# Linear attention with a squared-ReLU feed-forward on one core: a new token tiling, k.v in 64-row pairs, GpSimd taking early products, and a new order

## The chip, the core and the metric

The kernel runs on one core of a Trainium2 chip. A core has TensorE (PE: matmuls from SBUF into PSUM; its weight loads are shown apart as PEld), VectorE (DVE), ScalarE (ACT), GpSimd (POOL) and SyncE (SP, which here only issues DMAs), each with its own instruction stream, and 16 DMA engines that move data between DRAM and SBUF. The metric is the device time of one execution in microseconds (us), the median of the runs of a kernel.

## What is computed

Eight batches of eight heads, 576 tokens and 64 features per head go through an attention with an exponential feature map; its output, 4608 tokens of 512 features, goes through a feed-forward part.

```python
def phi(x):
    proj = np.einsum('bhsd,df->bhsf', x, w_phi)            # 64 -> 128
    proj = proj - np.max(np.abs(proj), axis=-1, keepdims=True)
    return np.concatenate([np.exp(proj), np.exp(-proj)], axis=-1)
q_p, k_p = (phi(q), phi(k))
kv = np.einsum('bhsf,bhsd->bhfd', k_p, v)
z = np.sum(k_p, axis=2)
num = np.einsum('bhsf,bhfd->bhsd', q_p, kv)
den = np.einsum('bhsf,bhf->bhs', q_p, z)[..., None] + 1e-06
attn = num / den
x = attn.transpose(0, 2, 1, 3).reshape(B * S, H * D)       # 4608 x 512
h = np.maximum(x @ w_in, 0.0)                              # 512 -> 2048
out = h * h @ w_out                                        # 2048 -> 512
```

Inputs and output are float32 in DRAM; the loads, issued by POOL, turn them into bfloat16 in SBUF.

## The kernel before

**Tiles of tokens.** A batch has 576 = 512 + 64 tokens per head. The 512 lie on the 128 partitions as token 4p + j (`load`, L245: runs of four tokens, 1024 bytes; `load_q`, L265: two halves of two tokens, 512 bytes). The last 64 tokens of each head are a part of their own ("s", L253), for two heads on the two halves of the partitions. From batch 2 on, the loads go out piece by piece (`PIECES`).

**Stages of a batch** (`attention(b)`).
- k and q are transposed. For the batches 0 and 1 PE does it (`pe_transposes`, L307, with a copy out of PSUM by DVE or ACT, L190 and L192); for the others SP issues a crossbar transpose in the DMA (`transposed`).
- `project` (L333; L360 for k of batch 0, L482 for q of batch 0) multiplies by `w_phi`, the token tile being the stationary operand. A matmul uses 64 of the 128 rows, one head; two heads stand on the two halves. DVE takes the maxima of the absolute values (L367, L388, L489), ACT the exponentials of k (L376, L394).
- The maxima of k go into v: ACT writes `exp(-max)` and `exp(max)` into two extra columns of `va` (`em_ops`, L407 and L413), DVE multiplies v by them (`v_ops`, L421).
- `kv_ops` multiplies `kp`, `kn` and `va`: per pair of heads 16 matmuls with 128 rows (tokens) and 65 columns (L449) and two with 130 columns for the part "s" (L454, on `va` columns of which half are zeros from a memset at the start). A copy takes the result to SBUF.
- `q_ops` projects q with `w_phi` as the stationary operand (L524), two exponentials follow (L539). In batch 0 all eight heads of 128 tokens are taken at once, which puts the eight matmuls on the same half of the rows.
- `out_ops` multiplies q's features with kv for eight heads (L554), positive part, scale by `en` on DVE (L566), negative part, reciprocal (L574), normalise into `xo` (L578). `xo` is transposed into `xT`: by PE in batch 0 (L594, copies L603), else by a DMA transpose that SP issues (L612). The 64 left tokens of a batch go to `xS`.

**Feed-forward.** Chunks 0 to 7 of 512 tokens are the batches' tiles, chunk 8 is `xS`. `ffn_in` (L692; `ffn_in_small`, L703, by 128 tokens in chunk 0) gives h, `relu_sq` takes it out of PSUM by ACT (L669) or DVE (L671), 512 columns each, and DVE squares it (L678). `ffn_out` (L757; L721 for the very last tile, in two halves) gives the output, a copy goes to `ot`, SP stores it (L772, L775).

**Order.** Every step is an `Op` with an engine; the functions only collect them. `ORDER` is the list of their numbers in the order of issue, and with it the order in each engine's stream; it was worked out ahead by a planner from the costs in `add`, and `STATES` says which of two engines takes an operation that `plan.either` offers to both. `BASES` gives the PSUM banks. `GATES` makes some loads wait for a named operation, `FILL` puts matmuls on a constant tile (L825) ahead of certain operations. `pin` ties each engine to this order. So the engines run in their own streams and wait for each other's results through semaphores.

Of the kernel before, what the change touches and what calls it, by code (L numbers as in the profile page):

```python
# [7 lines left out]
F32 = mybir.dt.float32  # L8
# [7 lines left out]
SEM = 0.045  # L16
# [8 lines left out]
def dve_cost(n):  # L25
    return n / 960 + 0.064, n / 960 + 0.150 + SEM

# [80 lines left out]
def kernel(  # L108
# [60 lines left out]
    kv_sb = ring("kv", 2, [4, 2, 2, D1])  # L169
    NQP = 3  # L170
    NXT = 2
    assert B * S == NCH * TCH and NCH == B + 1 and S == TCH + 64
# [3 lines left out]
    xT = [ring(f"xT{c}", 2, [4, 2, P]) for c in range(NXT)]  # L176
    xS = sb("xS", [4, KC, P])
    mkn = sb("mkn", [36], F32)
    hr = ring("hr", 4, [TCH])
# [13 lines left out]

    def ps1(g):
        return psum[:, g.base, :]
# [3 lines left out]


    PIECES = ((0, 1), (1, 2), (2, 3), (3, 4))

    LD = {"main": 2.85, "s": 0.3, "w": 2.85}

    def late(b, tag=""):
        return "ld" if b >= 2 else "v0" if b == 0 and tag == "xv" else "first"

    def work(b, x):  # L210

        return x + 0.1 if b >= 2 else x
# [21 lines left out]
    for b in range(2):  # L234
        for sg in range(2):
            def fn(b=b, sg=sg):
                pin(nc.vector.memset(va[b][sg][:, 32:40, :], 0.0))
            add("DVE", (0.49, 0.6), fn, w=[("ve", b, sg, 4, hi) for hi in range(2)], what="zero")

    def load(src, dst, b, tag, prs=((0, 4),), single=True, release=False):  # L240

        x = dst[b % 2]
        for a, z in prs:
            def fn(a=a, z=z):
                pin(nc.gpsimd.dma_start(  # L245
                    out=x[:, a * 512 : z * 512].rearrange("p (h x) -> p h x", x=4 * D),
                    in_=src[b][2 * a : 2 * z, 0:512, :].rearrange("h (p j) d -> p h (j d)", j=4)))
            add("POOL", (0.72, 0), fn, w=[(tag, b % 2, pr) for pr in range(a, z)],
                dma=(work(b, LD["main"] * (z - a) / 4), SW_IN, "ld", late(b, tag)), release=release, what=tag)
        if single:  # L250
            for hi in range(2):
                def fn(hi=hi):
                    pin(nc.gpsimd.dma_start(  # L253
                        out=x[hi * 64 : hi * 64 + 64, 2048:2304].rearrange("p (pr d) -> p pr d", d=D),
                        in_=src[b][hi::2, 512:576, :].rearrange("pr p d -> p pr d")))
                add("POOL", (0.72, 0), fn, w=[(tag, b % 2, "s", hi)], dma=(LD["s"], SW_IN, "ld", late(b)),
                    release=release, what=tag + "s")

    def load_q(b, jjs=(0, 1), single=True, release=False, prs=((0, 4),)):

        x = xq[b % 2]
        for jj in jjs:
            for a, z in prs:
                def fn(jj=jj, a=a, z=z):
                    pin(nc.gpsimd.dma_start(  # L265
                        out=x[:, jj * 1024 + a * 256 : jj * 1024 + z * 256].rearrange("p (h x) -> p h x", x=128),
                        in_=q[b][2 * a : 2 * z, 0:512, :].rearrange("h (p j) d -> p h (j d)", j=4)[:, :, jj * 128 : jj * 128 + 128]))
                add("POOL", (0.72, 0), fn, w=([("xq", b % 2, jj)] if z == 4 else []) + [("xq", b % 2, jj, y) for y in range(a, min(z, 3))],
                     dma=(work(b, LD["main"] / 8 * (z - a)), SW_IN, "ld", late(b)), release=release, what="xq")
        if single:  # L270
            load(q, xq, b, "xq", prs=(), release=release)

    def of(tag, b, us):
        qs = [("xq", b % 2, u, a) for u in us if u != "s" for a in range(3)] if tag == "xq" else []
        return qs + [(tag, b % 2, u) for u in us if u != "s"] + [(tag, b % 2, "s", hi) for u in us if u == "s" for hi in range(2)]

    def load_win(i):
        def fn():
            pin(nc.gpsimd.dma_start(
                out=win[i], in_=moe_w_in[:, i * 512 : (i + 1) * 512].rearrange("(kc p) m -> p kc m", p=P)))  # L280
        add("POOL", (0.72, 0), fn, w=[("win", i)], dma=(LD["w"], SW_IN, "ld", "first"), what="win")

    def load_wout(i):
# [3 lines left out]
        add("POOL", (0.72, 0), fn, w=[("wout", i)], dma=(LD["w"], SW_IN, "ld", "first"), what="wout")  # L287
# [6 lines left out]

    def attention(b):
        s2 = b % 2
        pe_in = b < 2
# [3 lines left out]
        def pe_transposes(x, tag, ttag, blocks, srcs, view):  # L301
# [6 lines left out]
            add("PE", pe_cost(n, 0.056), fn, r=of(tag, b, srcs) + ["ident"], opens=g, w=[g], what="T" + tag)  # L308
            def fn():
                i_ = ps1(g).bitcast(BF16)[:, : n * P].rearrange("p (i c) -> p i c", c=P)  # L310
# [4 lines left out]
        def transposed(x, xt, tag, ttag):  # L315
            def fn():
                pin(nc.sync.dma_start_transpose(out=xt, in_=x))
            add("SP", (2.8 if tag == "xk" else 3.4, 0), fn, r=of(tag, b, (0, 1, "s") if tag == "xq" else (0, 1, 2, 3, "s")),
                w=[(ttag, s2, t) for t in range(18)], dma=(3.6, HW_IN, "x", "kq"), what="X" + tag)
# [659 lines left out]
```

## Time and profile before

| | |
|---|---|
| median of 3 runs | 362.51 us (361.58 to 363.54) |
| span of the profiled execution | 358.8 us |
| granted clock of TensorE, mean | 0.997 |
| DMA queue of POOL (loads) | 51744 packets, 18.36 MB, 48.4% of 16 engines' span |
| DMA queue of SP (transposes, stores) | 50608 packets, 20.55 MB, 26.4% |
| POOL's own loads issued | 162, about 0.76 us each |

The span runs from the first to the last instruction of the profiled execution; the time of a run is longer, as it has the launch and the end around it. In the tables of groups a row gives line, engine, operation, operands and shapes, the number of instructions, their busy time in us, the mean of one in ns, and the idle time of the engine just before them with what ended it. A busy PE counts matmuls in flight, which overlap, so their mean (380 ns for 512 columns) is longer than the time from one start to the next (four L757 in 0.86 us). In tables by stretches, each engine has its busy time in that stretch and its number of instructions, then the granted clock, the DMA engines' busy share and GB/s. In the chain of waits and in the order of instructions, the first number is the start in us, the second the length.

### The profile page before, as it was taken

Reading aid. Unit: us, or ns where it says so; the run is one execution under the profiler, and the core shown is the slowest. Engines: PE = TensorE matmul, PEld = TensorE weight load, DVE = VectorE, ACT = ScalarE, POOL = GpSimd, SP = SyncE. Lnnn points to the kernel's source line nnn. Section 1 sums busy time; section 2 is a strip of 40 time slices with the busy share of each in tenths; the row PEclk is TensorE's granted clock in tenths of the full one; section 3 lists DMA queues with packets and bytes.
Section 4 is the critical chain, followed back from the end, with each engine's and each line's share of the span. In section 5 each row is a group of like instructions: output and inputs, shape, how many; then the busy total and the mean of one; then the engine's idle time right before and its main releaser. Section 6 shows DMA issues by size and latency. Waiting matters only on the chain.

```text
span 358.8 us, 8512 instructions
## 1 busy us (share of the span) xinstructions
PE 341.0 (95%) x3411; PEld 193.6 (54%) x3444; DVE 276.7 (77%) x525; ACT 227.1 (63%) x428; POOL 112.8 (31%) x167
## 2 busy tenths in 40 slices
PE   5989999979999999999999999999999998999994
PEld 4779975524554555455544644455555543444442
DVE  3999998869979997989778878799988816736210
ACT  3999887379779775796678577769777210340301
POOL 8845550784707930299301820000000000000000
PEclk9999999999999999999999999999999999999998
DMA  9999989999979998799956995600401121010105
GB/s 103 177 200 201 175 95 157 161 143 192 117 161 123 159 120 179 175 96 140 127 111 116 97 192 97 151 9 29 62 31 51 50 82 38 3 60 0 58 25 153
DMA packets 102631, 39.62 MB, mean 110 GB/s; under 512 B 77248, under 2 KB 98112, under 8 KB 102592
## 3 DMA queue, kind: packets, MB, share of 16 engines
q0 software_dynamic: 51744, 18.36, 48.4%
q1 hardware_dynamic: 50608, 20.55, 26.4%
q8 instruction: 27, 0.44, 0.5%
q10 hardware_dynamic: 240, 0.16, 0.2%
q14 instruction: 12, 0.10, 0.1%
HBM read 36.77 MB, written 9.44 MB: 129 GB/s over the span
## 4 chain that ended last, share of the span: by engine, by line
PE 72%; DVE 11%; ACT 9%; DMA 5%; issue 2%; SPq 0%; DVEq 0%; ACTq 0%; POOLq 0%
PE psum L757 27%; PE psum L692 24%; PE psum L554 5%; PE psum L333 4%; PE psum L703 3%; PE psum L449 3%; DVE va L421 3%; DMA out_dram<-ot 3%; PE psum L524 2%; ACT kp L394 2%; ACT kn L394 2%; DVE mq L489 2%; DVE h L678 2%; ACT hr L669 1%; DVE mk L367 1%
## 5 line engine op out<-in xcount | busy, mean ns | idle before, releaser
L757 PE MATMUL psum<-wout,h 128*128 128x512 bf16 x527 | 128.3, 380 | 2.5 <-issue 1.3
L692 PE MATMUL psum<-xT,win 128*128 128x512 bf16 x448 | 106.3, 379 | 3.9 <-ACT ot L192 2.5
L669 ACT ACTIVATE hr<-psum 128x512 bf16<-128x512 f32 x96 | 55.3, 596 | 48.2 <-PE psum L692 25.8
L757 PEld LDWEIGHTS <-h 128*128 128x128 bf16 x560 | 50.2, 98 | 54.3 <-issue 1.1
L692 PEld LDWEIGHTS <-win 128*128 128x128 bf16 x512 | 47.4, 97 | 58.0 <-issue 8.0
L678 DVE TENSOR_TENSOR h<-hr 128x512 bf16<-128x512 bf16 x144 | 56.4, 416 | 16.8 <-ACT hr L669 16.0
L539 ACT ACTIVATE qp<-psum 128x1024 bf16<-128x1024 f32 (+1 forms) x40 | 37.4, 940 | 23.1 <-PE psum L524 22.7
L265 POOL DMA_DIRECT2D xq<-in_q_dram x52 | 38.8, 764 | 33.8 <-ACT en L496 21.2
L489 DVE TENSOR_REDUCE mq<-psum 128x8 f32<-128x1024 f32 (+1 forms) x40 | 44.1, 1111 | 3.6 <-PE psum L333 2.9
L388 DVE TENSOR_REDUCE mk<-psum 128x8 f32<-128x1024 f32 (+1 forms) x35 | 38.2, 1111 | 3.1 <-PE psum L333 3.1
L671 DVE TENSOR_SCALAR hr<-psum 128x512 bf16<-128x512 f32 x48 | 32.8, 687 | 9.4 <-PE psum L692 7.9
L394 ACT ACTIVATE kp<-psum 128x1024 bf16<-128x1024 f32 (+1 forms) x35 | 32.8, 937 | 9.6 <-DVE mk L388 8.0
L539 ACT ACTIVATE qn<-psum 128x1024 bf16<-128x1024 f32 (+1 forms) x40 | 37.5, 940 | 1.5 <-PE psum L554 1.2
L394 ACT ACTIVATE kn<-psum 128x1024 bf16<-128x1024 f32 (+1 forms) x35 | 32.8, 937 | 0.0
L421 DVE TENSOR_TENSOR va<-xv,va 64x256 bf16<-64x256 bf16 (+2 forms) x68 | 30.4, 462 | 1.6 <-ACT va L413 0.8
L192 ACT ACTIVATE ot<-psum 128x512 f32<-128x512 f32 x18 | 10.7, 593 | 31.8 <-PE psum L757 27.3
L566 DVE TENSOR_TENSOR psum<-psum,en 128x520 f32<-128x520 f32 (+1 forms) x40 | 27.6, 698 | 3.8 <-PE psum L554 2.5
L578 DVE TENSOR_TENSOR xo<-psum,rden 128x512 bf16<-128x512 f32 (+1 forms) x40 | 27.4, 686 | 0.8
L245 POOL DMA_DIRECT2D xv<-in_v_dram x26 | 19.5, 757 | 23.3 <-DMA out_dram<-ot 20.8
L190 DVE COPY ot<-psum 128x512 f32<-128x512 f32 x17 | 11.6, 684 | 16.1 <-PE psum L757 9.4
L245 POOL DMA_DIRECT2D xk<-in_k_dram x28 | 21.1, 760 | 5.5 <-ACT va L407 3.5
L449 PE MATMUL psum<-va,kp 128*128 128x65 bf16 x256 | 19.6, 193 | 0.9 <-DVE va L421 0.4
(67 smaller groups left out, 402.4 us busy)
## 6 DMA issues: line engine op xcount, KB each, us to landing
out_dram<-ot SPq DMA_DIRECT2D x32, 256.0 KB, 2.8
xk<-in_k_dram POOLq DMA_DIRECT2D x26, 128.0 KB, 3.9
xq<-in_q_dram POOLq DMA_DIRECT2D x48, 64.0 KB, 3.9
xv<-in_v_dram POOLq DMA_DIRECT2D x24, 128.0 KB, 3.6
win<-in_moe_w_in_dram POOLq DMA_DIRECT2D x4, 512.0 KB, 11.7
wout<-in_moe_w_out_dram POOLq DMA_DIRECT2D x4, 512.0 KB, 9.4
xq<-in_q_dram POOLq DMA_DIRECT2D x4, 256.0 KB, 5.0
xv<-in_v_dram POOLq DMA_DIRECT2D x2, 512.0 KB, 9.1
```

Of the source, the lines that this page charges most:

```text
L245: pin(nc.gpsimd.dma_start(out=x[:, a * 512 : z * 512].rearrange("p (h x) -> p h x", x=4 * D), in_=src[b][2 * a : 2 * z, 0:512, :].rearrang ...
L265: pin(nc.gpsimd.dma_start(out=x[:, jj * 1024 + a * 256 : jj * 1024 + z * 256].rearrange("p (h x) -> p h x", x=128), in_=q[b][2 * a : 2 * z ...
L388: pin(nc.vector.tensor_reduce(out=mk_view(g), in_=ps2(pj)[:, :, : n * Fd].rearrange("p e (i f) -> p e i f", f=Fd), axis=AX.X, op=ALU.max, ...
L394: pin(nc.scalar.activation(out=dst[slot][:, :, :n, :].rearrange("p e i f -> p e (i f)"), in_=ps2(pj)[:, :, : n * Fd], func=ACT.Exp, scale= ...
L421: pin(nc.vector.tensor_tensor(out=t[:, :, :D].rearrange("p m (x c) -> p m x c", c=2), in0=x.rearrange("p (m x c) -> p m x c", m=n, c=2), i ...
L489: pin(nc.vector.tensor_reduce(out=mqb[:, c, :, :n], in_=ps2(pj)[:, :, : n * Fd].rearrange("p e (i f) -> p e i f", f=Fd), axis=AX.X, op=ALU ...
L539: pin(nc.scalar.activation(out=o, in_=i_, func=ACT.Exp, scale=sgn))
L669: pin(nc.scalar.activation(out=hr[sl], in_=ps1(g), func=ACT.Relu))
L671: pin(nc.vector.tensor_scalar(out=hr[sl], in0=ps1(g), scalar1=0.0, scalar2=None, op0=ALU.max))
L678: pin(nc.vector.tensor_tensor(out=dst, in0=i_, in1=i_, op=ALU.mult))
L692: pin(nc.tensor.matmul(out=o, lhsT=win[mc // 4][:, kc, mc % 4 * P : (mc % 4 + 1) * P], rhs=x, start=(kc == 0), stop=(kc == KC - 1)))
L757: pin(nc.tensor.matmul(out=ps1(g), lhsT=h2[c % 2][mc // 4][:, mc % 4, tt * P : (tt + 1) * P], rhs=wout[mc // 4][:, mc % 4, :], start=(mc = ...
```

## The change

- A head's 576 tokens lie as 9p + j on 64 partitions, two heads on the two halves; a run is nine tokens, 2304 bytes. The part "s" with its loads, memsets and products is gone. q comes in three loads, placed so that one token position j of all eight heads makes a tile; k and v come by head pairs, from batch 1 on by two pairs.
- `kv_ops` takes two head pairs with 72 matmuls of 64 rows and 65 columns; the two heads of a pair follow each other on the two halves of the rows and write different PSUM banks. One copy of 520 columns takes out the result of two pairs.
- q of batch 0 is projected like that of the others. Batch 1 is transposed by the crossbar (`PE_IN`). `en` is taken for several tiles at once.
- `xT` is one tile per batch, with one copy or one transpose per token tile.
- Squares are taken two at a time (1024 columns) except in chunk 0. In the first four batches and chunks (`LENT`) squares and products for v may go to POOL: `STATES` puts 24 squares and 3 products there.
- Stores go by 64 partitions, two for each output tile.
- `ORDER`, `BASES`, `STATES`, `GATES` (41 instead of 163) and `FILL` (90 matmuls instead of 120) are new. In the new order the very last tile is one that `ffn_out` copies whole; the one in two halves ends earlier.

```diff
+def pool_cost(n):
+    return n * 2.2e-3 + 0.15, n * 2.2e-3 + 0.25 + SEM
...
-    va = [[sb(f"va{b}{s}", [40, D1 + 1]) for s in range(2)] for b in range(2)]
+    va = [[sb(f"va{b}{s}", [36, D + 2]) for s in range(2)] for b in range(2)]
...
+    PE_IN, LENT = 1, 4
...
-    xT = [ring(f"xT{c}", 2, [4, 2, P]) for c in range(NXT)]
+    xT = ring("xT", 2, [4, KC, P])
...
+    def engine():
+        return nc.gpsimd if now[0].eng == "POOL" else nc.vector
...
+                o = x[:, a * 9 * D : z * 9 * D].rearrange("p (r x) -> p r x", x=9 * D)
+                i_ = src[b][2 * a : 2 * z].rearrange("(r h) (p j) d -> (h p) r (j d)", h=2, j=9)
+                pin(nc.gpsimd.dma_start(out=o, in_=i_))
...
+    def load_q(b, release=False):
+
+        x = xq[b % 2].rearrange("p (a x) -> p a x", a=2)
+        s = q[b].rearrange("(a u h) (p j) d -> u (h p) a (j d)", a=2, u=2, j=9)
+        for n, (u, lo, hi, to) in enumerate(((0, 0, 9, 0), (1, 0, 8, 10), (1, 8, 9, 9))):
+            def fn(u=u, lo=lo, hi=hi, to=to):
+                pin(nc.gpsimd.dma_start(out=x[:, :, to * D : (to + hi - lo) * D], in_=s[u][:, :, lo * D : hi * D]))
...
+                    pin(engine().tensor_tensor(
+                        out=t[:, :, :D].rearrange("p m (x c) -> p m x c", c=2),
+                        in0=xv[s2][:, 9 * a * D : 9 * z * D].rearrange("p (m x c) -> p m x c", m=n, c=2), in1=e, op=ALU.mult))
+                o = add("DVE", dve_cost(32 * n), fn, r=[("xv", s2, pr) for pr in range(a, z)] + [("ve", s2, sg, pr) for pr in range(a, z)],
+                        w=[("va", s2, sg, pr) for pr in range(a, z)], what="V")
+                if b < LENT:
+                    plan.either((o, "POOL", pool_cost(64 * n)))
...
+                    for pr in prs:
+                        for j in range(9):
+                            m = 9 * pr + j
+                            for sg in range(2):
+                                for hi in range(2):
+                                    r = slice(64 * hi, 64 * hi + 64)
+                                    pin(nc.tensor.matmul(
+                                        out=o[:, hi, pr % 2, sg, :],
+                                        lhsT=(kp, kn)[sg][kgroup[m // 8]][r, m % 2, m % 8 // 2, :],
+                                        rhs=va[s2][sg][r, m, :D1], start=(pr % 2 == 0 and j == 0 and sg == 0),
+                                        stop=(pr % 2 == 1 and j == 8 and sg == 1), skip_group_check=True))
...
+    def square(c, dst, src, n, r, w):
+        def fn():
+            pin(engine().tensor_tensor(out=dst, in0=src, in1=src, op=ALU.mult))
+        o = add("DVE", dve_cost(n // 2), fn, r=r, w=w, what="sq")
+        if c < LENT:
+            plan.either((o, "POOL", pool_cost(n)))
...
+            for u in range(2):
+                def fn(u=u):
+                    b, j = (2 * tt + u, 8) if c == NCH - 1 else (c, 2 * tt + u)
+                    o = out[b * S : b * S + S, :].rearrange("(p j) n -> j p n", j=9)[j]
+                    pin(nc.sync.dma_start(out=o, in_=ot[sl][u * 64 : u * 64 + 64, :]))
```

More of the change, by code (lines that the diff above doesn't have):

```diff
@@ L232, with load @@
     add("DVE", dve_cost(32), f_warm, w=["warm"], what="warm")
[L234 to L240, printed above, removed]
+    def load(src, dst, b, tag, prs=((0, 4),), release=False):
         x = dst[b % 2]
@@ L259, in load_q @@
[L259 to L271, printed above, removed]
@@ L469, in q_ts, with fn @@
[L469 to L472 removed]
+                def fn(sg=sg):
+                    pin(nc.scalar.activation(out=va[s2][sg][:, 9 * a : 9 * z, D:],
+                                             in_=mkb[:, 9 * a : 9 * z].to_broadcast([P, 9 * (z - a), 2]),
+                                             func=ACT.Exp, scale=(-1.0, 1.0)[sg]))
@@ L488, in fn @@
+            pj = project(qTb, "qT", ts, "Pq")
             def fn():
@@ L546, in out_ops @@
             g = Bank(2, "att")
-            whole = first or c == 4
-            head = [h if whole else 4 * (c % 2) + h % 4 for h in range(8)]
             def heads(sg):
```

390 lines of the change are left out of this document (150 added, 240 removed), and 176 rows, old and new, of tables (GATES, ORDER).

## The prediction

> **What bounds the kernel now.** I read the page's first rows, then the busy time by stretches, then the chain of waits, then the order of TensorE instructions in a few narrow windows.
>
> ```profile
> PE 341.0 (95%) x3411; PEld 193.6 (54%) x3444; DVE 276.7 (77%) x525; ACT 227.1 (63%) x428; POOL 112.8 (31%) x167
> PE 72%; DVE 11%; ACT 9%; DMA 5%; issue 2%; SPq 0%; DVEq 0%; ACTq 0%; POOLq 0%
> ```
>
> ```profile
> core 0: us, PE busy (x) PEld busy (x) DVE busy (x) ACT busy (x) POOL busy (x), PEclk, DMA share, GB/s
> 0.00:30.00 30.00, 24.50 (x397) 20.12 (x398) 23.86 (x55) 23.66 (x54) 20.83 (x33) 1.00 1.29 164
> 30.00:60.00 30.00, 29.39 (x509) 24.46 (x511) 27.95 (x57) 25.31 (x48) 12.64 (x18) 1.00 1.23 155
> 60.00:90.00 30.00, 27.12 (x223) 13.11 (x224) 25.50 (x44) 21.56 (x40) 19.37 (x29) 1.00 1.33 162
> 90.00:180.00 90.00, 88.35 (x943) 48.44 (x953) 79.99 (x144) 66.55 (x129) 48.34 (x71) 1.00 1.05 140
> 180.00:270.00 90.00, 88.94 (x857) 46.99 (x863) 77.50 (x139) 67.80 (x124) 11.65 (x17) 1.00 0.51 88
> 270.00:300.00 30.00, 28.66 (x225) 14.39 (x226) 17.01 (x39) 9.58 (x15) 0.00 (x0) 1.00 0.18 56
> ```
>
> TensorE (PE) is the bound after 30 us: from 30 to 300 us it is idle for 0.6 + 2.9 + 1.7 + 1.1 + 1.3 = 7.6 us only, most of it in two waits for the store of an output tile (the chain has DMA out_dram<-ot at 67.9 and 294.2). Before 30 us it is not: of its 24.5 busy us, 10.4 are L825, the filler. There VectorE (DVE) sets the pace:
>
> ```profile
> 20.60 1.63 DVE va L421 x5
> 22.89 2.27 DVE mq L489 x2
> 25.21 0.60 PE psum L524 x2
> 25.89 1.02 ACT qp L539
> 27.18 0.93 ACT qn L539
> 30.02 0.89 PE psum L703 x16
> ```
>
> L703 is the first product of the feed-forward part (f1). From there on PE has work enough. So the end is: the moment of the first f1, plus the PE work that is left by then, plus PE's idle time after it, plus what follows the last matmul.
>
> **Prices on PE**, from start to start in this window:
>
> ```profile
> 121.36 0.19 PE L449 MATMUL psum<-va,kn 128*128 128x65 bf16 x1
> 121.39 0.22 PE L454 MATMUL psum<-va,kp 128*128 128x130 bf16 x1
> 121.45 0.22 PE L454 MATMUL psum<-va,kn 128*128 128x130 bf16 x1
> 121.60 0.39 PE L524 MATMUL psum<-qT,wphi 64*128 64x512 bf16 x2
> 121.83 0.39 PE L333 MATMUL psum<-wphi,qT 64*128 64x128 bf16 x8
> 122.05 0.38 PE L524 MATMUL psum<-qT,wphi 64*128 64x512 bf16 x2
> 122.37 1.04 PE L692 MATMUL psum<-xT,win 128*128 128x512 bf16 x4
> ```
>
> 65 columns cost 0.030 us, 130 columns 0.057, 512 columns 0.216 (four L757 in 0.86), 128 columns 0.056 (16 L703 in 0.89). Two matmuls of 64 rows, on the upper and the lower half of the partitions, run as one: eight L333 take 0.22 us, four times 0.056, and two L524 take 0.23. Going from 128-row to 64-row matmuls or back costs 0.09 us (121.45 + 0.057 = 121.51, but L524 starts at 121.60; 122.05 + 0.216 = 122.27, L692 starts at 122.37). With these prices and the order list, before has 328.1 us of PE work, 14.0 of it ahead of the first f1 and 314.1 after it. 29.9 + 314.1 = 344.0; the last matmul ends at 354.3, so idle time and small gaps after 30 us are 10.3. Then 4.5 us of copy and store make 358.8, the span; the median of the runs lies 3.7 us above it.
>
> **The change, part by part.**
>
> *k.v by pairs (L449, L454).* Per batch 64 x 0.030 + 8 x 0.057 = 2.35 us go, 144 matmuls of 64 rows come, 72 pairs x 0.030 = 2.16: -1.5 us in eight batches. No row shows a pair of 65 columns. Bounds: 72 x 0.030, or, if no two matmuls follow each other faster than the mean of L333 (0.22 / 8 = 0.028 us each), 144 x 0.028 = 4.03, which is +13.4 us in all. I take the first, since in L333 it is the columns that set the time and not the number of instructions; the second is a rival. Changes between 64 and 128 rows, counted through both order lists: 110 before, 108 after, so nothing although k.v now is of the 64-row kind: the new order sets it beside projections.
>
> The Trainium skill, TensorE: Matmul & The Clock Gate (Wait — 56ns, not 53.3ns?), says that starts of matmuls never lie closer than about 25 ns, however short they are. By it 144 x 0.025 = 3.6 us a batch, +10 us in all. This trace disagrees for two row halves: L333 shows eight starts in 0.22 us only because each pair starts together, one pair every 56 ns; for pairs as short as 65 columns no run here shows it.
>
> *Batch 1 by crossbar, batch 0's q by pairs.* 36 PE transposes (L307) go: 36 x 0.056 = -2.0, with ten copies off DVE and ACT. Their two DMA transposes join SP's queue, ahead of the stores of chunk 0; kT<-xk and qT<-xq land 6.4 and 5.3 us after issue, and the new order puts eight f1 (8 x 0.9 = 7 us) before the first projection that needs them. Without that cover they would cost up to 6 us. In batch 0 the 32 single L482 become 16 pairs (-0.9) and eight single L524 four pairs (-0.9).
>
> Sum on PE: 328.1 - 1.5 - 2.0 - 1.8, less 0.4 for two changes of rows and rounding: 322.4. Ahead of the first f1 the new order has 8.6 of it (no batch 1 work, one tile's output instead of three), so 313.9 are left after it: as before.
>
> *The start.* DVE does ahead of the first f1, in the new order: 10 copies at 0.33 (ten halves and wholes, "0.94 DVE kT L190 x3" in the chain) = 3.3; 8 maxima at 0.60 ("1.20 DVE mk L367 x2") and 2 at 0.33 = 5.5; 7 products for v of 576 elements, 0.37 each ("1.63 DVE va L421 x5", 0.33 for 512 and fewer elements) = 2.6; 4 q maxima at 1.13 ("2.27 DVE mq L489 x2") = 4.5; scale, reciprocal, normalise, copy = 1.7. Sum 17.6. In the old order the same rows give 22.0: five q maxima, three tiles of output, products on 64 partitions. Both begin when the first k tile has been transposed, at 4.9. 4.9 + 22.0 = 26.9 against 29.9 measured, so 3.0 of waits; 4.9 + 17.6 + 3.0 = 25.5 for the new one. Between 23 (no waits) and 30 (loads late).
>
> *Loads.* Runs of 2304 bytes instead of 1024 and 512: per batch 512 + 512 + 768 runs instead of 5632. POOL issues 66 loads instead of 162, at 0.76 us each 73 us less. The time of the queue (48.4% of 358.8 = 174 us on each of 16 engines) falls with the runs to about 40% at best, or stays with the bytes. At the start I put it at nothing, as DVE is later. The four w_in loads move on POOL behind batch 0's nine loads, some of batch 1's and one product for v, which waits for the exponentials of the first head pair: in ACT's new order these stand behind twelve others, 0.48 apart in the trace from 6.4 on, so at some 13 us with a little waiting; before they were issued at 12.0 to 18.8 us and landed 11.7 later, the last about when f1 began. After 14 us four issues of 0.8 us still end before 18.8. If that product were late by more than a few us, f1 would be.
>
> *POOL sharing.* 24 squares and 3 products for v go to POOL. No row shows POOL doing one. Bounds: DVE's 0.42 for 512 elements, and 1.15 by the select of 128 columns (287 ns). I take the slow end: 1.15, 2.3 for 1024. DVE loses 24 squares; the rest come in twos (1024 elements at the 0.68 of L421's 128x1024 instead of 2 x 0.42): DVE falls by about 30 us, ACT by some 15 (fewer and longer copies, exponentials by head pairs). Neither bounds, so this is worth only what it takes off PE's idle time.
>
> ```profile
> L678 DVE TENSOR_TENSOR h<-hr 128x512 bf16<-128x512 bf16 x144 | 56.4, 416 | 16.8 <-ACT hr L669 16.0
> L421 DVE TENSOR_TENSOR va<-xv,va 128x1024 bf16<-128x1024 bf16 x28 | 19.0, 681 | 1.1 <-ACT va L413 0.8
> L782 POOL TENSOR_SCALAR_AFFINE_SELECT ident<-ident 128x128 bf16<-128x128 bf16 x1 | 0.3, 287 | 0.1
> ```
>
> *Idle time after the first f1.* 10.3 before. The stores wait less behind loads (the 6.3 us store at 67.9 stood in a queue busy 1.33 by the windows), DVE is less full. Bounds 3 and 13; I take 7.8, two and a half less, one of the two long waits.
>
> *The end.* The last tile now is copied whole (0.60 instead of 0.38) and stored by two issues one behind the other on SP (0.5 more): 4.5 + 0.7 = 5.2.
>
> **Sum:** 25.5 + 313.9 + 7.8 + 5.2 = 352.4, plus 3.7: 356.
>
> **Rivals.**
>
> *Pairs limited by the number of matmuls.* The mechanism and price of above: 144 x 0.028 instead of 2.16 us a batch, 15 us over my sum: 371. For it: nothing in the trace is faster than 0.028 on average. Against: pairs in L333 start together. It makes the change slower once a pair costs more than 0.041 us (0.011 x 72 x 8 = 6.4 us, the forecast's gain).
>
> *POOL holds DVE up.* 13 of the 27 products lie in the first 50 us, where DVE is 93% busy (27.95 of 30): 13 x 1.15 = 15 us of POOL. If DVE stands for half of that, h2 and the next batch are 7.5 us late and PE waits for them: 363.5. Against it: most of DVE's work reads PSUM. The Trainium skill, GPSIMD Engine Reference (Key points), says that GpSimd shares its SBUF interfaces with VectorE and contends with instructions that have two SBUF inputs; this is the rival it speaks for, and before, with no product on POOL, cannot show it.
>
> *More than forecast.* First f1 at 23, idle 4, all else as above: 346.1 + 3.7 = 350. For it: DVE has little left to wait for when loads come in longer runs. Against: the first k tile decides as before.
>
> **Chances.** Forecast 0.60, pairs limited 0.15, POOL holds DVE 0.14, more than forecast 0.11. A measurement of this kernel tells 0.5%, 1.8 us, from no change. The forecast's own range, 351 to 360, is faster throughout; the second rival is split between same and slower. Faster 0.71, same 0.09, slower 0.20. The range 347 to 367 leaves out most of the first rival and a little below.
>
> **What would show it.** First f1 at 25 to 26; starts of 65-column pairs 30 ns apart; 18 k.v blocks of 0.54 us a head pair; POOL products of 1.2 and 2.4 us, DVE squares of 1024 elements at 0.68 and no longer while POOL works; PE idle from 30 to 300 us near 5. It is wrong if pairs lie at 50 ns or more, if f1 comes at 29 or later, or if PE's idle time grows beyond 13.

## The result and the profile after

The changed kernel takes 390.3 us (median of four runs, 383.7 to 393.5) against 362.0 beside it: ratio 1.070, interval 1.058 to 1.082. Ratios and their intervals, here and below, leave out runs more than 1.5% above the fastest of their kernel (392.0 and 393.5 here), so that 390.3 / 362.0 is not the ratio. The forecast was 356, with a range of 347 to 367. The profiled execution has a time of 383.7 and a span of 381.8 us.

First the page of the changed kernel: busy time by engine, then busy tenths and granted TensorE clock in 40 slices of 9.5 us, then the queues and the chain that ended last.

```profile
PE 342.7 (90%) x3922; PEld 192.9 (51%) x3954; DVE 258.0 (68%) x388; ACT 221.2 (58%) x380; POOL 88.7 (23%) x98
...
PE   8579169978999599999997999999999999999994
...
PEclk9889769998999989999998999999999999999999
...
q0 software_dynamic: 19488, 18.35, 32.9%
q1 hardware_dynamic: 55792, 21.74, 29.3%
...
PE 71%; DMA 17%; DVE 4%; issue 3%; ACT 2%; POOL 1%; SPq 0%; DVEq 0%
```

TensorE is busy for almost the same time as before (341.0 then), but the span is 23 us longer: it waits, and DMA's share of the chain has gone from 5% to 17%. The fifth slice (38 to 48 us) is nearly empty, and in it and the next the granted clock is down to 0.7 and 0.6. The mean clock of the profiled execution is 0.964; it was 0.997 before.

Busy time by stretches says how much (columns as in the prediction's table: five engines, granted clock, DMA share, GB/s):

```profile
0.00:27.00 27.00, 19.92 (x375) 16.72 (x375) 18.39 (x39) 19.73 (x43) 17.64 (x29) 0.93 1.11 177
27.00:60.00 33.00, 21.65 (x361) 20.14 (x360) 18.81 (x28) 15.10 (x29) 15.58 (x17) 0.80 1.24 179
60.00:215.00 155.00, 140.62 (x1768) 74.77 (x1778) 116.81 (x164) 104.73 (x173) 54.72 (x52) 0.97 0.79 133
```

and the kernel before, from 60 us on:

```profile
60.00:215.00 155.00, 150.11 (x1485) 79.72 (x1501) 134.30 (x243) 113.79 (x210) 79.36 (x116) 1.00 1.06 141
```

The first f1 starts at 26.6 us. From 27 to 60 us TensorE idles for 33 - 21.65 = 11.4 us, from 60 to 215 for 14.4; before, it idled for 4.9 us in the same 155. The waits of TensorE (us in total, times, longest):

```profile
PE psum L316 <- DMA kT<-xk: 12.1, 2, 11.3
PE psum L621 <- DMA xT<-xo: 6.9, 2, 3.7
PE psum L476 <- DVE mq L443: 2.4, 1, 2.4
```

The longest is batch 1's projection of k (L316). The chain of waits into it:

```profile
16.17 12.95 DMA xk<-in_k_dram
29.12 0.02 issue
29.14 21.80 DMA kT<-xk
50.93 0.05 issue
50.98 1.25 PE psum L316 x20
52.23 4.47 PE psum L637 x64
```

Batch 1's second k load lands 12.95 us after its issue, and the crossbar transpose that waits for it takes 21.8 us to land. The 64 matmuls of f1 (L637) behind the wait take 4.47 us instead of the 3.57 that 0.0558 us each gives: until 53.9 us the granted clock is 0.50. On SP's queue the same place reads (start, duration of the issuing instruction):

```profile
29.14 10.67 SPq L300 DMA_TRANSPOSE kT<-xk  x1
39.91 13.06 SPq L300 DMA_TRANSPOSE qT<-xq  x1
53.15 5.71 SPq L300 DMA_TRANSPOSE kT<-xk  x1
```

The issuing instruction itself holds SP for 10.67 and 13.06 us; the third, with fewer loads beside it, for 5.71. What ran beside them I counted from the trace's packets, per 5 us on all 16 engines of the core:

```
us        transposes (256 B)   loads (1024 and 1152 B)
35 to 40         607                  588
40 to 45         738                  701
45 to 50         753                  719
50 to 55        1180                  528
55 to 60        2854                    5
```

While loads run, about one transpose packet goes for one load packet. From 35 to 55 us a transpose packet takes 31 ns (median; 18 where no loads run), a load packet 96 (1024 bytes) or 106 (1152 bytes). From 40 to 50 us about 150 pairs go per us; on 16 engines that is a pair in 107 ns, about as long as a load packet. So a load packet's duration sets the transpose's pace. From 55 us on, without these loads, four times as many transpose packets go. The Trainium skill, DMA: Bandwidth & Descriptors (Queues, rings and completion order), says that each DMA engine goes round the queues that have work and switches between them by packets. The counts above agree with it.

### The profile page after: what moved, and what is told of

It is laid out like the page before. It is cut to its first block, busy times and chain, and to the rows that moved or that the text cites. A ratio compares the mean times of both kernels' runs of the same rounds, so it can differ in the third digit from the quotient of the medians.

```text
span 381.8 us, 9343 instructions
## 1 busy us (share of the span) xinstructions
PE 342.7 (90%) x3922; PEld 192.9 (51%) x3954; DVE 258.0 (68%) x388; ACT 221.2 (58%) x380; POOL 88.7 (23%) x98
## 3 DMA queue, kind: packets, MB, share of 16 engines
q0 software_dynamic: 19488, 18.35, 32.9%
q1 hardware_dynamic: 55792, 21.74, 29.3%
## 4 chain that ended last, share of the span: by engine, by line
PE 71%; DMA 17%; DVE 4%; issue 3%; ACT 2%; POOL 1%; SPq 0%; DVEq 0%
PE psum L696 27%; PE psum L621 26%; DMA kT<-xk 7%; PE psum L504 4%; PE psum L421 4%; PE psum L316 4%; DMA xk<-in_k_dram 3%; DMA xT<-xo 3%; PE psum L637 2%; DMA qT<-xq 2%; PE psum L476 2%; DMA out_dram<-ot 2%; PE psum L759 2%; DVE mq L443 1%; PE psum L660 1%
## 5 line engine op out<-in xcount | busy, mean ns | idle before, releaser
L597 ACT ACTIVATE hr<-psum 128x512 bf16<-128x512 f32 x91 | 52.7, 599 | 59.5 <-PE psum L621 50.7
L621 PEld LDWEIGHTS <-win 128*128 128x128 bf16 x512 | 48.4, 99 | 65.6 <-issue 14.7
L605 DVE TENSOR_TENSOR h<-hr 128x1024 bf16<-128x1024 bf16 (+1 forms) x56 | 41.0, 743 | 16.0 <-ACT hr L597 15.5
L599 DVE TENSOR_SCALAR hr<-psum 128x512 bf16<-128x512 f32 x53 | 36.1, 688 | 13.0 <-PE psum L621 10.3
L605 POOL TENSOR_TENSOR h<-hr 128x512 bf16<-128x512 bf16 (+1 forms) x24 | 35.5, 1494 | 22.8 <-DVE hr L599 12.6
L196 ACT ACTIVATE ot<-psum 128x512 f32<-128x512 f32 x20 | 11.8, 596 | 31.3 <-PE psum L696 20.6
L194 DVE COPY ot<-psum 128x512 f32<-128x512 f32 x15 | 10.3, 687 | 24.1 <-PE psum L696 18.2
L244 POOL DMA_DIRECT2D xq<-in_q_dram x24 | 17.5, 736 | 35.9 <-ACT kn L377 10.7
L402 DVE TENSOR_TENSOR va<-xv,va 128x1152 bf16<-128x1152 bf16 (+1 forms) x33 | 21.9, 698 | 5.3 <-ACT va L389 4.6
L234 POOL DMA_DIRECT2D xv<-in_v_dram x16 | 11.7, 728 | 51.8 <-ACT kv L196 18.4
L316 PE MATMUL psum<-wphi,kT 64*128 64x128 bf16 x252 | 12.0, 224 | 12.9 <-DMA kT<-xk 12.1
```

The source lines that it names most:

```text
L316: pin(nc.tensor.matmul(out=o[:, e, i * Fd : (i + 1) * Fd], lhsT=xt[r, t, :], rhs=wphi2[r, :], start=True, stop=True))
L597: pin(nc.scalar.activation(out=view, in_=ps1(g), func=ACT.Relu))
L599: pin(nc.vector.tensor_scalar(out=view, in0=ps1(g), scalar1=0.0, scalar2=None, op0=ALU.max))
L605: pin(engine().tensor_tensor(out=dst, in0=src, in1=src, op=ALU.mult))
L621: pin(nc.tensor.matmul(out=o, lhsT=win[mc // 4][:, kc, mc % 4 * P : (mc % 4 + 1) * P], rhs=x, start=(kc == 0), stop=(kc == KC - 1)))
```

## The experiments

Thirteen kernels were run, each with three timed rounds beside the kernel before, in four sets. Kernels of different sets are compared by their ratios, those of one set by medians too. A *stall* is a gap between two matmuls beyond their price; as it is counted from start to start, it can be 0.1 to 0.2 us longer than the idle time in the profile.

**Set 1: what is the first stall, and is it all?** Batch 1's k and q by TensorE again; ten transpose groups and their evacuations are set between f1s by hand:

```diff
-    PE_IN, LENT = 1, 4
+    PE_IN, LENT = 2, 4
```

> Batch 1 is transposed on PE again (ten groups of transposes and their copies put between the f1 of chunk 0), all else as in the changed kernel. Theory A (batch 1's crossbar transposes, run among the weight loads, are what PE waits for): the 11.4 us stall at 39.5 us and the half-clock stretch behind it go, 2.0 us of PE work come back; 11.4 + 3.5 - 2.0 = 13 us faster than the changed kernel's 383.7 to 388.6, so 371 to 376; what the later batches lose stays. Theory B (POOL's products hold DVE up and that starves PE): no more than 3 us faster.

Measured: 386.0 us (384.7 to 388.1), ratio 1.064, 1.058 to 1.070. The 11 us stall is gone and the last f1 of chunk 0 starts at 60.0 instead of 66.8 us. But the time misses the 371 to 376 that theory A expected, and the ratio can't be told from the changed kernel's. The first f1 of chunk 1 (F1 from here on) starts at 82.9 (87.5 in the changed kernel), that of chunk 4 at 214.3 (214.1): the head start is used up by then. The longest waits are now on the transposes of xT:

```profile
PE psum L621 <- DMA xT<-xo: 10.1, 4, 5.0
PE psum L288 <- DMA xq<-in_q_dram: 3.5, 1, 3.5
PE psum L476 <- DVE mq L443: 3.3, 2, 3.0
```

Next, the two loads of batch 1 that the transposes wait for (operations 20 and 21 of `ORDER`) go ahead of w_in, nothing else:

```diff
-    66, 44, 57, 67, 50, 22, 46, 58, 68, 47, 52, 59, 12, 70, 69, 76, 60, 61, 23, 53, 51, 78, 62, 56, 75, 63, 65, 80,
+    49, 66, 44, 57, 67, 50, 22, 46, 58, 68, 47, 52, 59, 12, 70, 69, 76, 60, 61, 23, 53, 51, 20, 21, 78, 62, 56,
...
-    20, 127, 37, 108, 104, 27, 128, 101, 81, 21, 109, 117, 119, 90, 129, 102, 89, 26, 110, 105, 103, 25, 111, 118,
+    88, 55, 85, 94, 73, 127, 37, 108, 104, 27, 128, 101, 81, 109, 117, 119, 90, 129, 102, 89, 26, 110, 105, 103,
```

> Only the second k load and one q load of batch 1 move ahead of the four w_in loads in POOL's order. Theory A in its narrow form (load packets and transpose packets take turns one for one on each DMA engine): the k transpose starts near 15 us but still has to share with w_in: 144 packets per engine at 98 + 18 ns = 16.7 us, so it lands at 32 to 34, about when PE wants it; the stall shrinks from 11.4 to 0 to 3 us, f1 comes 1 to 2 us later; 372 to 378. Rival (the k load was merely late, and a transpose takes 6.6 us as in the later batches): it lands by 23.

Measured: 392.4 us (390.6 to 394.5), ratio 1.081, 1.075 to 1.086, where 372 to 378 us were expected. The kT transpose is issued at 19.45 us instead of 29.14, and the crossbar is no faster (it lands after 20.7 us):

```profile
19.45 9.63 SPq L300 DMA_TRANSPOSE kT<-xk  x1
29.18 16.65 SPq L300 DMA_TRANSPOSE qT<-xq  x1
```

The stall at 39 us turns into one of 5.8 us at 51 us for q, and others of 4.9 and 5.3 us follow. An early start didn't help a transpose that meets w_in's packets in place of later ones.

The loads of w_in, w_out and batch 1's k and v in two halves each (512 to 640 byte packets, twice as many):

```diff
-                pin(nc.gpsimd.dma_start(out=o, in_=i_))
+                for lo, hi in ((0, 5 * D), (5 * D, 9 * D)) if b == 1 else ((0, 9 * D),):
+                    pin(nc.gpsimd.dma_start(out=o[:, :, lo:hi], in_=i_[:, :, lo:hi]))
...
+            for u in range(2):
+                m = i * 512 + u * 256
```

> The loads of w_in, w_out and of batch 1's k and v go out in two halves each, so that their packets have 512 to 640 bytes instead of 1024 and 1152; everything else is the same. If packets take turns one for one, batch 1's k transpose needs 144 x (60 + 18) ns = 11.2 us and about 2 for issue and landing instead of 21.8, and PE's stall falls from 11.4 us to 2 to 5; 376 to 382. If the transposes only wait for a share of the bandwidth by bytes, it stays at 20 us or more and the time at 384 to 390.

Measured: ratio 1.085, 1.076 to 1.095 (391.6 to 399.7 us), where 376 to 382 us were expected. The transposes do get on faster beside shorter packets:

```profile
30.27 7.30 SPq L306 DMA_TRANSPOSE kT<-xk  x1
37.67 9.82 SPq L306 DMA_TRANSPOSE qT<-xq  x1
```

7.30 and 9.82 us instead of 10.67 and 13.06, the transpose lands in 15.9 us instead of 21.8, and the stall is 7.9 us instead of 11.4. From 45 to 48 us 702 transpose packets go for 700 load packets (median 59 ns), 234 a us instead of 150: still one for one, and faster as the load packets are shorter. In time it is no gain: stalls of 3.7, 4.9 and 5.7 us follow it.

All 27 products that GpSimd takes back to VectorE (a 1 in STATES is an operation on its second engine):

```diff
 STATES = (
...
-    '0000001000000000000000011101001100101010101011011000101001111110000010011000000110010001110110001011'
-    '0010000101011001011100100000010010101110110001000100001101110000100010000000000101101110010010110111'
+    '0000000000000000000000011001001100000000000001010000000001010100000010001000000110010001010100001001'
+    '0010000101010000011000000000000010101100110000000000001101100000100010000000000101101110010010110111'
```

> All 27 products that POOL takes go to DVE; order and all else as in the changed kernel. Theory A: the stall at 39.5 us stays within 1 us and the time within 1% of the changed kernel (383 to 392). Theory B: DVE's long squares (up to 2.2 us beside a POOL product, against 0.69) go, and the time falls by 4 us or more.

Measured: 391.9 us (391.2 to 394.5), ratio 1.081, 1.076 to 1.086, as theory A expected; its longest wait is the same:

```profile
PE psum L316 <- DMA kT<-xk: 13.3, 2, 11.4
```

GpSimd's share is not the cause of the slowdown. What it does cost shows in the changed kernel's trace: of seven VectorE products beside one of GpSimd's four are longer and three are not, and instructions that read PSUM keep their time. The four lose 4.6 us in all, 2.2 of it in one product ahead of the long stall:

```profile
37.23 0.69 DVE L599 TENSOR_SCALAR hr<-psum 128x512 bf16<-128x512 f32 x1
37.84 0.41 DVE L194 COPY xT<-psum 128x512 bf16<-128x512 bf16 x1
38.17 2.65 DVE L605 TENSOR_TENSOR h<-hr 128x512 bf16<-128x512 bf16 x1
```

2.65 us where this form takes 0.42 alone, while the copy and the relu beside the same GpSimd products keep their 0.41 and 0.69. What decides is who started first. The four long ones started while a GpSimd product was running (this one at 38.17, GpSimd's at 38.05) and end 0.6 to 0.8 us after one of GpSimd's ends. The three others had started before GpSimd's, by 0.16, 0.16 and 0.38 us, and there GpSimd's own product is the longer one: 1.15, 2.27 and 2.05 us, where most take 1.04 (512 elements) and 1.9 (1024).

**Set 2: where does the head start of e1_pe1 go?** Each of these is e1_pe1 with one thing more. In its trace VectorE waits for xo buffers that transposes still read, F1 waits for xT, and DMA stands still from 55 to 60 us and is busy again from 65 us on (share 0.76 and more by 5 us). Five xo buffers, and five of the reciprocals that go with them:

```diff
-    xo = ring("xo", 3, [8 * D])
-    rden = ring("rden", 3, [8], F32)
+    xo = ring("xo", 5, [8 * D])
+    rden = ring("rden", 5, [8], F32)
...
-            xs = xslot[0] % 3
+            xs = xslot[0] % 5
```

> Batch 1 on TensorE (as e1_pe1, 386.0 us) and five xo buffers instead of three. In e1_pe1 VectorE's L528 waits 4.8 us in all, three times, for an xT transpose that still reads its buffer (the longest 3.5 us, at 121.8 us), and what is behind it on VectorE waits too. Theory C (the rest of the loss is transposes and stores that hold buffers and chunks up): 381 to 384 us, stall of 5.1 us at 125.8 us shorter by 3 or more. Theory O (the new order is paced by something else, and a head start is always given back): 385 to 388 us.

Measured: 385.3 us (383.3 to 390.0), ratio 1.065, 1.060 to 1.071: no gain. The first F1 of chunk 2 starts 2 us earlier (128.9), that of chunk 4 at 213.5.

The first four xT tiles of batches 1 and 2 by TensorE:

```diff
-            if first:
+            if first or (b in (1, 2) and c < 4):
                 g2 = Bank(1, "tp")
```

> As e1_pe1, and the first four xT tiles of batches 1 and 2 are transposed by TensorE (eight L540 groups of four with eight evacuations) instead of by the crossbar. This adds 1.8 us of TensorE work and takes the DMA landing (6.3 us and 3.4 us in e1_pe1) out of the way of the first F1 of chunks 1 and 2. Theory C: the stalls of 4.0 us at 78.7 and 5.1 us at 125.8 shrink to under 1.5 us each, with the halved clock behind them: 373 to 378 us. Theory O: 384 to 388 us, first F1 of chunk 4 still at about 214 us.

Measured: 387.2 us (385.0 to 390.7), ratio 1.073, 1.065 to 1.081. Both waits for xT are gone as expected, yet nothing is gained; another crossbar transpose, batch 3's kT, now comes late:

```profile
92.39 3.63 PE L621 MATMUL psum<-xT,win 128*128 128x512 bf16 x16
102.50 1.03 PE L316 MATMUL psum<-wphi,kT 64*128 64x128 bf16 x16 [6.48 <-DMA kT<-xk]
```

```profile
88.43 7.45 SPq L300 DMA_TRANSPOSE kT<-xk  x1
95.99 2.28 SPq L549 DMA_TRANSPOSE xS<-xo  x1
98.44 5.65 SPq L300 DMA_TRANSPOSE qT<-xq  x1
```

This kT is issued at 88.4, amid the loads that the planner's gates let go from 76 us on, and lands 14.0 us later.

All gates off (the changed kernel's list has 42 entries, that of the kernel before 131):

```diff
 GATES = {
-    338: 149, 339: 139, 340: 166, 341: 122, 342: 216, 343: 277, 344: 251, 508: 278, 509: 379, 510: 458, 511:
...
 }
```

> As e1_pe1, without the planner's gates that hold the loads of batches 2 to 7 back: GpSimd issues each as soon as its buffer is free and its place in the queue comes. Theory G (loads that were held back until 70 to 90 us run against the xT transposes, while DMA stands still from 54 to 62 us): loads fill 54 to 62 us, xT lands in 2.5 to 3.5 us instead of 6.3 us at 76.5 us, 377 to 382 us. Theory C without G: loads now meet other transposes, kT and qT above all: 385 to 393 us.

Measured: 385.9 us (384.4 to 388.0), ratio 1.069, 1.063 to 1.075. DMA is busy from 55 to 62 us now (share 0.78), but GpSimd issues seven more loads from 71.8 to 76.8 us, and xT, issued from 71.0 on, lands in 8.2 us (median of four). So one wait is longer:

```profile
PE psum L621 <- DMA xT<-xo: 9.9, 3, 8.1
```

Both together (its diff is the two above):

> xT of batches 1 and 2 by TensorE as e7_xtpe, and no gates as e8_gates. Theories C and G together: 366 to 374 us. C alone: as e7_xtpe within 3 us. Theory O: 383 to 390 us.

Measured: 375.6 us (374.0 to 376.0), ratio 1.039, 1.034 to 1.044. Neither edit alone moves the time; together they take the ratio from e1_pe1's 1.064 to 1.039, 9 us, a little less than theories C and G expected. That fits two causes in series: while either kind of late transpose is left, it takes the time that the other gave back.

**Set 3: how much is it in all?** e9_both with batch 1 on the crossbar, as the change has it:

```diff
-    PE_IN, LENT = 2, 4
+    PE_IN, LENT = 1, 4
```

> As e9_both, but with batch 1's k and q by crossbar, as the change has them: the 11.4 us stall should be back at about 39 us. If the head start that TensorE's transposes of batch 1 give is kept once the later collisions are out of the way (theory C): 382 to 389 us, 7 to 13 us over e9_both's 375.6. If it is given back anyway (theory O): 374 to 379 us.

Measured: 381.0 us (380.0 to 381.8), ratio 1.057, 1.049 to 1.064: 5.4 us over e9_both by the medians, 6.5 by the ratios, and a little under what was expected. The stall is back, 13.0 us at 38.8 us; the first F1 of chunk 1 is 8.0 us later, that of chunk 4 5.4. TensorE's longest wait:

```profile
PE psum L316 <- DMA kT<-xk: 15.0, 2, 12.9
```

Then the loads themselves, cut to 128 bytes a packet (part of the computation is left out). First e1_pe1 so:

```diff
+                if b >= 2:
+                    o, i_ = o[:, :, :D], i_[:, :, :D]
...
+                hi = lo + 1 if b >= 2 else hi
```

> As e1_pe1 (batch 1 on TensorE, gates as the change has them), and the loads of q, k and v of batches 2 to 7 fetch the first 64 of every 576 columns only: as many DMA issues and packets, of 128 bytes instead of 1024 and 1152; the rest of the buffers keeps older data, so that part of the computation is left out. All instructions of the engines stay as they are. Theories C and G (crossbar transposes and stores wait for the packets of loads beside them): kT, qT, xT and stores of batches 2 to 7 land in under 4 us, the stalls of 4.0, 5.1 and 3.0 us go, and so does the halved clock behind them: 366 to 375 us. Theory O (the order itself is too tight, whatever the DMA does): 382 to 387 us.

Measured: ratio 1.034, 1.022 to 1.046 (369.7 to 374.9 us in the three runs that it goes by). Nothing but the loads differs from e1_pe1 (1.064): as many packets, those cut with an eighth or a ninth of their bytes. 3% or 11 us go. Theory O falls: it is not the order by itself that holds the kernel at 385.

Then e9_both with the same loads:

> As e9_both (xT of batches 1 and 2 by TensorE, no gates), with the shortened loads of e14_light for batches 2 to 7 (part of the computation is left out there). What is left of collisions in e9_both (its stalls of 2.5, 2.9 and 1.4 us and the clock behind them) goes: 364 to 371 us by theories C and G; 374 to 377 us by theory O. What then remains above 362 us is the first 60 us (w_in, w_out and batch 1's loads are whole) and the cost of the order itself.

Measured: ratio 1.028, 1.020 to 1.037 (369.8 to 371.2 us in the three runs that it goes by). 371 is at the expected range's upper end, 4 us under e9_both, though the two intervals overlap a little.

**Set 4: batch 1 with the loads beside it shortened.** The changed kernel, and e1_pe1, with w_out's loads cut too; the second product reads w_in's tiles in place of w_out's:

```diff
-                out=wout[i], in_=moe_w_out[i * 512 : (i + 1) * 512, :].rearrange("(kc p) n -> p kc n", p=P)))
+                out=wout[i][:, :, :D], in_=moe_w_out[i * 512 : (i + 1) * 512, :D].rearrange("(kc p) n -> p kc n", p=P)))
```

> The changed kernel as it is (batch 1 by crossbar, its gates), with the shortened loads of e14_light for batches 2 to 7 and w_out's loads shortened in the same way (first 64 of 512 columns; the second product reads w_in's tiles in its place, so that part of the computation is left out). Batch 1's own loads and w_in's are whole. Theory C (batch 1's transposes were late because the packets of w_out and of later loads took turns with theirs): the 21.8 us landing of the second kT falls under 10 us, the stall of 11.4 us under 3 us, and the crossbar's saving of TensorE work (2 us) shows: 366 to 373 us, not above e18_e1light by more than 1 us. Rival (the crossbar is late for batch 1 whatever runs beside it, since the loads of batch 1 itself come too late): stall of 7 us or more, 376 us or more.

> As e1_pe1 (batch 1 on TensorE), with the same shortened loads as e17_aflight, w_out's among them. Theory C: like e14_light or up to 3 us faster, 368 to 374 us. Its difference from e17_aflight is the worth of batch 1's crossbar with few loads beside it: predicted -2.0 us; by the rival +5 us or more.

Measured: 364.8 us (363.6 to 364.9) for the first, ratio 1.010, 1.006 to 1.014, a little under the expected range; 372.6 us (370.1 to 376.1) for the second, ratio 1.030, 1.023 to 1.037. With the loads cut, and the same instructions on every engine, the changed kernel falls from 1.070 to 1.010 of the time before, 6% or 21 us. Its queue q0 still has 19488 packets, with 7.28 MB instead of 18.35. In e17_aflight SP's queue and TensorE's waits read:

```profile
29.34 6.08 SPq L303 DMA_TRANSPOSE kT<-xk  x1
35.52 6.08 SPq L303 DMA_TRANSPOSE qT<-xq  x1
41.79 3.75 SPq L303 DMA_TRANSPOSE kT<-xk  x1
```

```profile
PE psum L291 <- DMA xq<-in_q_dram: 3.3, 1, 3.3
PE psum L319 <- DMA kT<-xk: 3.0, 1, 3.0
PE psum L624 <- DMA xT<-xo: 2.6, 2, 1.6
```

The same kT, issued at the same moment (29.3), holds SP for 6.08 us instead of 10.67 and lands in 12.4 instead of 21.8; the stall is 3.0 us instead of 11.3. It did not fall under 10 and 3 us as expected: batch 1's own q and v loads, whole here, run beside it until 35 us. And batch 1's crossbar is now a gain: by the ratios 7 us under e18_e1light, where the forecast had 2.0. The last f1 starts 1.9 us earlier, as the crossbar's saving of TensorE work would have it; the rest comes later, where e18_e1light waits 6.1 us in all for xT and e17_aflight 2.6. Why these differ was not followed up; e18_e1light's groups were placed by hand and not by the planner, which may be part of it.

The stretches of the profiled executions side by side (idle is the stretch less TensorE's busy time; for the kernel before, the first stretch is 30 to 60 us; the last two columns are the starts of the first F1 of a chunk):

| | ratio | idle 27-60 | idle 60-215 | mean clock | F1 of chunk 1 | F1 of chunk 4 |
|---|---|---|---|---|---|---|
| before | 1 | 0.6 | 4.9 | 0.997 | 74.9 | 189.0 |
| changed | 1.070 | 11.4 | 14.4 | 0.964 | 87.5 | 214.1 |
| e1_pe1 | 1.064 | 2.4 | 16.8 | 0.962 | 82.9 | 214.3 |
| e9_both | 1.039 | 2.9 | 13.5 | 0.981 | 80.8 | 205.7 |
| e10_b1x | 1.057 | 13.2 | 12.2 | 0.970 | 88.8 | 211.1 |
| e18_e1light | 1.030 | 2.3 | 8.7 | 0.979 | 80.5 | 200.3 |
| e17_aflight | 1.010 | 3.3 | 4.7 | 0.979 | 76.5 | 194.0 |

e1_pe1 shows where a head start can go. Of the 9 us that it no longer idles from 27 to 60 us, 2.4 come back as idle time from 60 to 215. The rest goes into longer work: TensorE is busy for 350.6 us instead of 342.7, of which 2 us are batch 1's transposes. Behind its stalls at 79 and 126 us the granted clock is 0.50 for 6.8 us each (81.9 to 88.7 and 129.7 to 136.5), in the changed kernel for 3.4 each.

## Why the prediction was wrong

**The start: right.** First f1 at 26.6, forecast 25.5 (23 to 30). Here a miss was made up elsewhere: the first 55 fillers ran at 107 ns each (half clock) until 6.1 us, so that the first transpose started at 6.5 us, not at the 4.9 counted on:

```profile
1.07 5.61 PE L759 MATMUL psum<-warm 128*128 128x128 bf16 x55 [1.07 <-DVE warm L219]
6.52 0.39 PE L288 MATMUL psum<-ident,xk 128*128 128x128 bf16 x4
```

**k.v by pairs: right, and its rival fell.** 64-row matmuls of 65 columns start in pairs 30 ns apart at full clock; 36 pairs (72 matmuls) take 1.09 us:

```profile
108.82 0.19 PE L421 MATMUL psum<-va,kp 64*128 64x65 bf16 x2
108.85 0.20 PE L421 MATMUL psum<-va,kn 64*128 64x65 bf16 x2
108.89 0.19 PE L421 MATMUL psum<-va,kp 64*128 64x65 bf16 x2
108.92 0.19 PE L421 MATMUL psum<-va,kn 64*128 64x65 bf16 x2
```

The number of matmuls doesn't limit them. The mean of 15 ns per matmul lies under the 25 ns that the Trainium skill, TensorE: Matmul & The Clock Gate (Wait — 56ns, not 53.3ns?), gives as the floor, so for two row halves the trace differs from that rule, and the trace decides. (A slip in the prediction's sum changes nothing: 64 x 0.030 + 8 x 0.057 is 2.38, not 2.35, 0.2 us in eight batches.)

**GpSimd's sharing: sized right, and its rival fell.** Products of 512 elements took 1.05 us (1.15 forecast), of 1024 1.94 (2.3). VectorE lost 4.6 us to them, not 7.5, and e5_nopool shows no gain without them. VectorE's busy time fell by 18.7 us (276.7 to 258.0) and ScalarE's by 5.9, not by 30 and 15; the prediction took neither for a bound, and TensorE's longest wait for either is 2.4 us.

**The end: right.** 5.0 us behind the last matmul (it ends at 376.7), forecast 5.2:

```profile
373.75 2.97 PE L696 MATMUL psum<-wout,h 128*128 128x512 bf16 x13
```

**Batch 1 by crossbar: this step failed.** The prediction had two landing times of 6.4 and 5.3 us from the trace of before and set eight f1, 7 us, against them: "Without that cover they would cost up to 6 us." The cover was there, and the landing took 21.8 us, because the row it was priced by is a median over transposes that met few or short loads: three of before's six kT ran beside no load at all, and the slowest of them (8.3 us) had most of its packets go from 82 to 84 us, 1600 for 226 load packets of 128 bytes. At 29 us w_out's loads and those of q, k and v keep the queue full: a DMA share of 1.24 from 27 to 60 us in the stretches above. Before it was as full there (1.23 from 30 to 60 us in the prediction's table), but no transpose of k or q was issued before 51.7 us; that one landed in 10.9 us, twice the median. So the price was in no row; it should have been bounded from above, by the packets that share the engines, and not taken as known. What the crossbar of batch 1 cost can't be told apart from nothing as the change stands (1.070 against e1_pe1's 1.064, their intervals overlap), since later stalls take up the difference; with those out of the way it is +5 to +7 us (e10_b1x against e9_both, intervals apart), where -2.0 was forecast.

**Loads at nothing: failed with it.** The prediction counted runs and bytes, and asked whether loads come in time. It did not ask what longer packets do to the other queue. Queue q0 moved 18.36 MB in 51744 packets before, 355 bytes each, and 18.35 MB in 19488 now, 942 bytes each. At the price it was after, that worked: its share fell from 48.4% to 32.9%. But one packet of a transpose goes for one load packet, and load packets of 1024 and 1152 bytes take 96 to 107 ns. That the length sets the pace is shown by e2_small, where the bytes are the same. That loads beside transposes make up most of the 7% is shown by e17_aflight, where 21 us go; as it cuts bytes with the length, it doesn't say how much of the 21 us is length alone, and e2_small, which halves the length of the early loads only, gained nothing.

**Idle time after the first f1: failed, as the sum of these.** Forecast 7.8 (bounds 3 and 13), one of two waits for a store taken off 10.3; those two are 2.5 and 1.2 us, about half and not most of the 7.6 idled before. Measured: from the first f1 at 26.6 to the last matmul's end at 376.7 are 350.1 us. TensorE idles for 11.35 + 14.38 + 1.21 = 26.9 of it (the last from 215 us on) and is busy for 323.2, which is 9.3 more than the 313.9 that the prediction priced. So the term is 36.2 us instead of 7.8, and this is the whole error of the span but 1 us: 28.4 + 1.1 (start) - 0.1 (end) = 29.4 = 381.8 - 352.4. In e17_aflight the same count gives 3.29 + 4.65 + 0.55 = 8.5 idle, close to the forecast's number; its span of 361.7 is above 352.4 mostly by the start (1.4) and by work that took 7.6 us longer than its price, some of it at slow clock (0.95 from 27 to 60 us, 0.96 from 90 to 130).

**A term that was missing: the clock.** All prices came from a trace with the clock at 1.00 in every stretch. A stall costs its length and then some of the work behind it at half clock. In the long one the clock falls 3.9 us after TensorE went idle (39.7) and is full again 2.9 us after it resumed:

```profile
43.62:50.95 7.33, 0.00 (x0) 0.00 (x0) 0.00 (x0) 0.00 (x0) 0.00 (x0) 0.50 1.21 197
50.98:53.86 2.88, 2.88 (x37) 2.68 (x38) 1.82 (x2) 1.67 (x3) 0.33 (x1) 0.50 1.21 194
```

After the first f1 the granted clock is 0.50 in five stretches, 24 us in all, 7.5 of them inside stalls; the other 16 us of work so cost about 8 more than at full clock. That is most of the 9.3 us above. The Trainium skill, TensorE: Matmul & The Clock Gate (What's actually happening), puts the gate's window at about 3.4 us of idling. This trace agrees in that the clock falls 3.9 us into the stall of 11.3 us and that e9_both, without a stall over 1 us between 27 and 60 us, has 1.00 there. Shorter gaps close together bring it too: in e9_both the clock is 0.50 from 76.7 to 80.0 us, where the longest gap shortly before was 1.0 us and TensorE had been busy for 3.2 us from 71.0 to 76.6.

What stays open: e17_aflight, with its loads cut, is still 1% slower than before (1.006 to 1.014). It has a stall of 3.4 us at 10.9 us for batch 0's q load, 3.0 us for kT, and the slow clock behind both; none was taken out by itself. The kernel before was not run with its loads cut, so part of the 21 us might come off it as well; it idles for only 0.6 + 4.9 us between 30 and 215 us, at full clock. No version beat the kernel before; e9_both is the fastest that computes everything.

## What to carry to other kernels

A transfer's landing time holds only for the traffic that ran beside it. Before moving a crossbar transpose, or lengthening the packets of loads, look at what the queue carries at the new place; where it is full, expect a transpose of 256-byte packets to take as many load packets as it has its own, times a load packet's duration. Here that is 144 on each engine, at about 105 ns 15 of the 21.8 us.

When taking out the longest stall gives nothing back, take out the next of the same kind together with it before calling the first harmless: here two edits were worth nothing singly and 9 us together. A quick bound on the sum is to cut the traffic that is suspected and leave every instruction in place; do the same to the kernel before, to know what of it belongs to the change.

Price a stall with the clock behind it: here the 3 to 6 us after a stall of 3 us or more ran mostly at half clock.

## What the hardware showed that was not expected

Transposes and loads went nearly packet for packet (738 to 701 in 5 us; 702 to 700 in 3 us beside packets of half the length), so that the length of the *other* queue's packets set a transpose's pace; and the issuing instruction on SP lasts for much of that time, 10.7 and 13.1 us, holding the transposes and stores queued behind it.

Beside GpSimd products VectorE's two-input SBUF products took up to 2.65 us instead of 0.42, but only in the four of seven overlaps in which GpSimd had started first; in the other three GpSimd's product was longer. All forms that read PSUM kept their time. The Trainium skill, GPSIMD Engine Reference (Key points), has the contention for instructions with two SBUF inputs; that the one that starts second waits is what this trace adds.
